# Decode kernel, attention plus MLP on one core: w1 becomes the first load and the hidden vector h is computed ahead of q

## The chip, the core and the metric

The kernel runs on one core of a Trainium2 chip. A core has five engines that run side by side, each with its own instruction queue: PE (matrix products into PSUM; "PEld" is its weight load), DVE (vector work), ACT (activations), POOL (here only constants), and SP, which here only issues transfers. Engines wait for each other by semaphores. Sixteen DMA engines move data between the chip's main memory and the on-chip memory SBUF. The metric is the time of one execution in microseconds (us), lower is better; the figure for a kernel is the median of several executions.

## What is computed

One token (x, 1024 values) goes through a layer norm, and the result xn feeds two branches whose sums are added to x:

```python
def _A_ref(x, k_cache, v_cache, wq, wo):      # 32 query heads, 4 kv heads, head size 128
    W = min(4096, max(256, Sk // 4))          # 4096: the last 4096 cached positions
    q = (x @ wq) ...                          # wq 1024 x 4096
    scores = einsum("bhqd,bhkd->bhqk", q, k) * (Dh ** -0.5)
    p = softmax(scores)
    o = einsum("bhqk,bhkd->bhqd", p, v)
    return o.reshape(B, Sq, Hq * Dh) @ wo     # wo 4096 x 1024
def _B_ref(x, w1, b1, w2, b2):
    h = gelu(layernorm(x) @ w1 + b1)          # w1 1024 x 3584
    return h @ w2 + b2                        # w2 3584 x 1024
xn = layernorm(x)
return x + _A_ref(xn, ...) + _B_ref(xn, ...)
```

All inputs are bfloat16. The six big ones take 38 MiB: wq 8, K 4, V 4, w1 7, w2 7, wo 8. Each is read once, and there is one token, so there is little arithmetic for each byte.

## The kernel before

**Where the data lies.** SBUF has four large tiles, which are used more than once. WA holds wq, and later w2; the end of WA, past w2, also holds the softmax numerators Pb and their transpose PT. W1 holds w1, and later rows 0 to 27 of wo (each "row" c is one slice of 128 x 1024). KT holds K, and later the last four rows of wo; V holds V. A small scratch tile of the gelu, HT32, lies in the last part of KT in the kernel before.

**Loads.** All large loads are issued by SP, one after the other (`load_rows`, L148-154, is one transfer per chunk): wq first (L156); then SP waits for a POOL constant (L187) and issues K in two halves (L188-192), w1 (L193), V in two halves (L194-198). Then it waits until PE has finished the product that gives q (L298) and issues w2 over wq (L299); then it waits until PE has finished h (L385) and issues wo in six chunks of 16, 8, 4, 2, 1 and 1 rows (L386-387). ACT issues x and b1 early (L169-170) and b2 (L245).

**Order of the work, in the order of each engine's queue.**

1. Layer norms (L240-278): xn goes to XNTb, the second norm to YTb.
2. `wide_product` (L281-294): 64 matmuls; each group of four runs side by side on four column strips of PE. With wq it gives q (L296).
3. q is copied, transposed and spread to QB (L301-324).
4. DVE transposes K in place, four pieces (L326-331); PE multiplies each piece by QB as it comes (scores, L339-348).
5. Softmax: maximum over PSUM (L352), a few tiny steps, exp on ACT (L367), the transpose PT on DVE (L370), sums and reciprocals (L373-381).
6. `wide_product` with w1 gives h (L384); DVE and ACT add b1, transpose, and apply gelu to GT (L389-413).
7. p times V (32 matmuls, L425-429), normalise (L432-440), spread to OT (L443-448); x and b2 are added by four matmuls (L453-455).
8. `bulk` (L457-461) multiplies one row of weights as two matmuls that run side by side. All 28 rows of w2 come first (L463-469), then rows 0 to 27 of wo (L476), then the last four rows in smaller pieces (L480-484).
9. DVE copies the sums (L488-492), adds (L495), and SP stores the result (L497).

PE takes its instructions in this order, whatever data is there.

## Time and profile before

| | |
|---|---|
| median of 3 executions | 101.97 us (101.0 to 102.63) |
| profiled execution, its own time | 100.91 us |
| its span, first to last instruction | 99.6 us |
| moved by DMA | 39.89 MB, mean 400 GB/s over the span |
| PE busy | 48.4 us (49%) |
| DVE busy | 38.8 us (39%) |
| ACT, POOL busy | 6.6 us, 9.6 us |

The profile comes from one execution. It has a page (busy shares, the span in 40 slices, DMA queues, the chain of work that ended last, the costliest groups of instructions, DMA issues) and a trace that can be asked for a timeline, for the waits of each engine, or for stretches of time ("windows"). L289 is line 289 of the kernel; "WA<-in_A_wq_dram" means that WA is written from that input. In the trace, the tile W1 is called W, and w1 and w2 both come as "in_B_w_dram". "PEclk" is the granted clock of PE, 1 being full speed.

### The profile page before, as it was taken

What the parts mean: (1) busy time and instruction counts of PE and PEld (TensorE: products, weight loads), DVE (VectorE), ACT (ScalarE), POOL (GpSimd) and SP (SyncE); (2) the same over time, 40 slices, a digit from 0 to 9 for tenths busy, and PEclk for the clock granted to TensorE, in tenths of its full rate; (3) what the DMA queues carried; (4) which work ended last, traced back from release to release, by engine and by line L of the source; (5) the groups of instructions that cost most, each with busy time, mean ns of one, the idle gap of its engine ahead of it and who ended that gap; (6) DMA issues with size and microseconds to landing.
All of it is one profiled execution on the core that took longest, in us unless ns stands there. A gap on an engine that the chain in (4) does not pass through costs nothing.

```text
span 99.6 us, 859 instructions
## 1 busy us (share of the span) xinstructions
PE 48.4 (49%) x350; PEld 19.3 (19%) x350; DVE 38.8 (39%) x50; ACT 6.6 (7%) x11; POOL 9.6 (10%) x40
## 2 busy tenths in 40 slices
PE   0000220008973419756071179990800899795760
PEld 0000220003321003112020133540700223241210
DVE  4000443000027999999918175498100000000052
ACT  0000236000022000000000620000000000000000
POOL 5777720000000000000000000000000000000000
PEclk9999999999999555599999755999555558999999
DMA  9199999939999889998699999999889999999920
GB/s 421 79 474 553 423 474 474 447 132 428 428 441 651 368 368 391 529 529 375 253 428 428 434 510 414 483 553 391 368 368 431 421 414 421 414 424 390 382 100 1
DMA packets 1906, 39.89 MB, mean 400 GB/s; under 512 B 224, under 2 KB 240, under 8 KB 624
## 3 DMA queue, kind: packets, MB, share of 16 engines
q1 hardware_dynamic: 1880, 39.85, 93.9%
q8 instruction: 2, 0.03, 0.1%
q10 hardware_dynamic: 24, 0.01, 0.0%
HBM read 39.86 MB, written 0.00 MB: 400 GB/s over the span
## 4 chain that ended last, share of the span: by engine, by line
DMA 52%; DVE 25%; PE 17%; ACT 2%; issue 1%; SPq 0%; DVEq 0%
DMA W<-in_A_wo_dram 30%; DMA WA<-in_A_wq_dram 22%; DVE KT L331 17%; PE PS L289 12%; DVE MX L352 2%; ACT WA L367 2%; PE PS L345 2%; DVE BULK L492 2%; DVE TQ L307 1%; PE PS L459 1%; DVE Q L302 1%; DVE QB L322 1%; SPq L150 0%; DVE ORow L495 0%; PE PS L311 0%
## 5 line engine op out<-in xcount | busy, mean ns | idle before, releaser
L331 DVE STREAM_TRANSPOSE KT<-KT 128x4096 bf16<-128x4096 bf16 x4 | 17.4, 4412 | 0.0
L345 PE MATMUL PS<-KT,QB 128*128 128x512 bf16 x32 | 9.7, 459 | 8.7 <-DVE KT L331 8.7
L459 PE MATMUL PS<-WA,GT 128*1 128x512 bf16 x56 | 9.0, 498 | 5.1 <-DMA WA<-in_B_w_dram 5.1
L492 DVE COPY BULK<-PS 1x256 f32<-1x256 f32 x4 | 1.7, 417 | 23.4 <-PE PS L459 23.3
L289 PE MATMUL PS<-WA,XNTb 128*32 128x512 bf16 x64 | 6.5, 592 | 7.9 <-DMA WA<-in_A_wq_dram 7.9
L459 PE MATMUL PS<-W,OT 128*1 128x512 bf16 x56 | 6.5, 378 | 2.5 <-DMA W<-in_A_wo_dram 2.5
L252 PE MATMUL PS<-XT,onesf 128*128 128x16 f32 x2 | 0.6, 386 | 11.7 <-DVE XT L249 11.7
L345 PEld LDWEIGHTS PS<-KT,QB 128*128 128x128 bf16 x32 | 3.3, 112 | 15.6 <-DVE KT L331 11.5
L302 DVE CAST Q<-PS 128x512 bf16<-128x512 f32 x1 | 0.7, 692 | 13.1 <-PE PS L289 13.1
L289 PE MATMUL PS<-W,YTb 128*32 128x448 bf16 x64 | 5.4, 525 | 0.0
L459 PEld LDWEIGHTS PS<-WA,GT 128*1 128x1 bf16 x56 | 2.9, 104 | 10.9 <-issue 9.3
L289 PEld LDWEIGHTS PS<-WA,XNTb 128*32 128x32 bf16 x64 | 2.4, 142 | 11.6 <-DMA WA<-in_A_wq_dram 8.0
L241 DVE STREAM_TRANSPOSE XT<-XB 128x256 bf16<-128x256 bf16 x1 | 0.6, 625 | 8.5 <-DMA XB<-in_A_x_dram 8.5
L427 PE MATMUL PS<-V,WA 128*64 128x512 bf16 x32 | 3.6, 380 | 0.0
L459 PEld LDWEIGHTS PS<-W,OT 128*1 128x1 bf16 x56 | 2.2, 83 | 6.9 <-DMA W<-in_A_wo_dram 2.8
L367 ACT ACTIVATE WA<-PS,NMB 128x2048 bf16<-128x2048 f32 x1 | 2.0, 1967 | 23.3 <-DVE NMB L365 23.3
L444 PE MATMUL PS<-ON,E 128*128 128x32 f32 x8 | 1.9, 404 | 2.8 <-DVE ON L439 2.8
L370 DVE STREAM_TRANSPOSE WA<-WA 128x2048 bf16<-128x2048 bf16 x1 | 2.3, 2312 | 2.1 <-ACT WA L367 2.1
L352 DVE TENSOR_REDUCE MX<-PS 128x1 f32<-128x2048 f32 x1 | 2.3, 2291 | 2.0 <-PE PS L345 2.0
L289 PEld LDWEIGHTS PS<-W,YTb 128*32 128x32 bf16 x64 | 2.2, 138 | 3.0 <-issue 2.8
L252 PEld LDWEIGHTS PS<-XT,onesf 128*128 128x128 f32 x2 | 0.5, 312 | 11.7 <-DVE XT L249 11.7
L215 POOL TENSOR_SCALAR_AFFINE_SELECT E<-E 32x512 f32<-32x512 f32 x4 | 2.5, 629 | 0.6
(87 smaller groups left out, 37.3 us busy)
## 6 DMA issues: line engine op xcount, KB each, us to landing
W<-in_B_w_dram SPq DMA_DIRECT2D x1, 7168.0 KB, 45.2
WA<-in_B_w_dram SPq DMA_DIRECT2D x1, 7168.0 KB, 48.1
KT<-in_A_k_cache_dram SPq DMA_DIRECT2D x2, 2048.0 KB, 25.6
V<-in_A_v_cache_dram SPq DMA_DIRECT2D x2, 2048.0 KB, 51.6
W<-in_A_wo_dram SPq DMA_DIRECT2D x1, 4096.0 KB, 23.5
W<-in_A_wo_dram SPq DMA_DIRECT2D x1, 2048.0 KB, 28.0
W<-in_A_wo_dram SPq DMA_DIRECT2D x1, 1024.0 KB, 30.0
KT<-in_A_wo_dram SPq DMA_DIRECT2D x1, 512.0 KB, 30.8
```

What stands on the lines that cost most here:

```text
L215: p(pool.affine_select(out=ap, in_=ap, pattern=[[1, 4], [-1, 128]], compare_op=ALU.not_equal, fill=1.0, base=0, channel_multiplier=4))
L289: last = pe.matmul(PS[32 * a:32 * a + 32, banks[b] * 512: banks[b] * 512 + n], lhsT=vec[:, k:k + 1].to_broadcast([128, 32]), rhs=weights[: ...
L302: d(dve.tensor_copy(Q4[:, 0:512], bank(4)))
L331: C["kt"].append(d(dve.transpose(KT[:, lo:lo + W], KT[:, lo:lo + W])))
L345: last = pe.matmul(bank(nb), lhsT=QB[:, G * 512 + c * 128:G * 512 + (c + 1) * 128], rhs=kg[:, c, 16 * nb:16 * nb + 16, :], start=False, st ...
L352: C["mx"] = d(dve.tensor_reduce(out=MX[:, :], in_=PS[:, 0:2048], axis=AX.X, op=ALU.max))
L367: C["exp"] = ACT.mark(act.activation(out=Pb, in_=PS[:, 0:2048], func=ACTF.Exp, bias=NMB[:, 0:1], scale=SCALE, accum_out=RS[:, 0:1]))
L370: C["PT"] = d(dve.transpose(PT, Pb))
L427: last = pe.matmul(PS[64 * q:64 * q + 64, 3 * 512:4 * 512], lhsT=PT[:, t * 64:(t + 1) * 64], rhs=vb[:, t], start=(t < 2), stop=(t >= 30))
L444: last = pe.matmul(bank(2, 352, 32), lhsT=E4[:, dq * 128:(dq + 1) * 128], rhs=ON[:, dq * 32:(dq + 1) * 32], start=(dq == 0), stop=(dq == 3))
L459: ins = pe.matmul(PS[32 * q:32 * q + 1, 6 * 512:7 * 512], lhsT=vec[:, c:c + 1], rhs=weights[:, lo + q * 512: lo + (q + 1) * 512], start=fi ...
L492: d(dve.tensor_copy(BULK[32 * a:32 * a + 1, :], PS[32 * q:32 * q + 1, lo:lo + 256]))
```

## The change

The order of the loads becomes w1, wq, K, V, w2, wo, and h with its gelu is computed before q. w1 takes the first place in SP's queue; wq is issued after the wait for the POOL constant, then K. The product h and the whole chain to GT move ahead of the product q, on PSUM banks 0 and 1 instead of 4 and 5. HT32 moves from KT to the same place in V, so SP waits for DVE's copy out of HT32 (C["ht"]) before it issues V. Then SP waits for q and issues w2, and behind it (h is long done) wo rows 0 to 27; it then waits for the scores (C["sc"]) and issues the last four rows of wo into KT. Everything from p times V on keeps its place and order.

```diff
-    HT32 = KT[:, 3 * W:3 * W + 2 * QW].bitcast(f32)
+    HT32 = V[:, 3 * W:3 * W + 2 * QW].bitcast(f32)
...
-    load_rows(WA, wq_p, WQ_CHUNKS, NQ, s_wq)
+    load_rows(W1, w1_p, W1_CHUNKS, F, s_w1)
...
     sp.wait_ge(POOL.sem, C["selq"])
+    load_rows(WA, wq_p, WQ_CHUNKS, NQ, s_wq)
     for G in range(NP):
         sp.dma_start(
             KT[:, G * PW:(G + 1) * PW],
...
-    load_rows(W1, w1_p, W1_CHUNKS, F, s_w1)
-    for G in range(NP):
-        sp.dma_start(
-            V[:, G * PW:(G + 1) * PW],
...
+    pe.wait_ge(DVE.sem, C["y"])
+    wide_product(W1, W1_CHUNKS, F, s_w1, YTb, QW // 2, [0, 1], "h")
+    dve.wait_ge(PE.sem, C["h"])
+    dve.wait_ge(s_b1, 16)
+    d(dve.tensor_tensor(
+        out=HW32[:, :].rearrange("p (b n) -> p b n", b=2),
+        in0=PS[:, 0:2 * 512].rearrange("p (b n) -> p b n", b=2)[:, :, 0:QW // 2],
+        in1=B1R[:, :].rearrange("p (b n) -> p b n", b=2), op=ALU.add))
+    dw()
+    d(dve.transpose(HT32[:, :].rearrange("p (c i) -> p c i", c=FC),
+                    HW32[:, :].rearrange("p (j c) -> p c j", c=FC)))
+    dw()
+    C["ht"] = d(dve.tensor_copy(HT[:, :], HT32[:, 0:QW:32]))
...
+    C["GT"] = d(dve.tensor_tensor(out=GT[:, :], in0=HT[:, :], in1=U2[:, :], op=ALU.mult))
+
+    sp.wait_ge(DVE.sem, C["ht"])
+    for G in range(NP):
+        sp.dma_start(
+            V[:, G * PW:(G + 1) * PW],
...
     wide_product(WA, WQ_CHUNKS, NQ, s_wq, XNTb, 512, [4, 5], "q")
 
     sp.wait_ge(PE.sem, C["q"])
     load_rows(WA, w2_p, W2_CHUNKS, D, s_w2)
+    sp.wait_ge(PE.sem, C["h"])
+    load_rows(W1, wo_p, WO_CHUNKS[:3], D, s_wo[:3])
...
     C["sc"] = PE.mark(last)
+    sp.wait_ge(PE.sem, C["sc"])
+    load_rows(KT, wo_p, WO_CHUNKS[3:], D, s_wo[3:], first=WO_BULK)
...
-    wide_product(W1, W1_CHUNKS, F, s_w1, YTb, QW // 2, [4, 5], "h")
-    sp.wait_ge(PE.sem, C["h"])
-    load_rows(W1, wo_p, WO_CHUNKS[:3], D, s_wo[:3])
-    load_rows(KT, wo_p, WO_CHUNKS[3:], D, s_wo[3:], first=WO_BULK)
...
```

The lines removed behind the last one shown are the same chain from L389 to L413 that is added further up.

More of the change, by code (lines that the diff above doesn't have):

```diff
@@ L192, in bass_parallel_sum__sliding_block_cached__mixer_channel_mlp__decode_kernel @@
         ).then_inc(s_k[G], 16)
-    load_rows(W1, w1_p, W1_CHUNKS, F, s_w1)
-    for G in range(NP):
-        sp.dma_start(
-            V[:, G * PW:(G + 1) * PW],
-            A_v_cache[0, 2 * G:2 * G + 2, SK - W:SK, :].rearrange("g (m b) d -> m g (b d)", m=64),
-        ).then_inc(s_v[G], 16)
     p(pool.memset(ML[:, :], NEG))
@@ L294, in wide_product @@
         C[name] = PE.mark(last)
+    pe.wait_ge(DVE.sem, C["y"])
[11 more added lines that the diff above has]
+    C["ht"] = d(dve.tensor_copy(HT[:, :], HT32[:, 0:QW:32]))
+    dw()
+    d(dve.tensor_tensor(out=U2[:, :], in0=HT[:, :], in1=HT[:, :], op=ALU.mult))
+    dw()
+    C["d_T"] = d(dve.scalar_tensor_tensor(out=U2[:, :], in0=U2[:, :], scalar=1.0 / 0.044715, in1=HT[:, :],
+                                          op0=ALU.add, op1=ALU.mult))
+    act.wait_ge(DVE.sem, C["d_T"])
+    C["a_sig"] = ACT.mark(act.activation(out=U2[:, :], in_=U2[:, :], func=ACTF.Exp,
+                                         scale=-GELU_C * 0.044715))
+    dve.wait_ge(ACT.sem, C["a_sig"])
+    d(dve.tensor_scalar(out=U2[:, :], in0=U2[:, :], scalar1=1.0, scalar2=None, op0=ALU.add))
+    dw()
+    d(dve.reciprocal(out=U2[:, :], in_=U2[:, :]))
+    dw()
+    C["GT"] = d(dve.tensor_tensor(out=GT[:, :], in0=HT[:, :], in1=U2[:, :], op=ALU.mult))
[3 more added lines that the diff above has]
+            V[:, G * PW:(G + 1) * PW],
+            A_v_cache[0, 2 * G:2 * G + 2, SK - W:SK, :].rearrange("g (m b) d -> m g (b d)", m=64),
+        ).then_inc(s_v[G], 16)
     wide_product(WA, WQ_CHUNKS, NQ, s_wq, XNTb, 512, [4, 5], "q")
@@ L381, in bass_parallel_sum__sliding_block_cached__mixer_channel_mlp__decode_kernel @@
         out=RR4[:, :].rearrange("o (q m) -> o q m", q=4), in_=LR[:, :].unsqueeze(1).to_broadcast([1, 4, 32])))
-    wide_product(W1, W1_CHUNKS, F, s_w1, YTb, QW // 2, [4, 5], "h")
-    sp.wait_ge(PE.sem, C["h"])
-    load_rows(W1, wo_p, WO_CHUNKS[:3], D, s_wo[:3])
-    load_rows(KT, wo_p, WO_CHUNKS[3:], D, s_wo[3:], first=WO_BULK)
-    dve.wait_ge(PE.sem, C["h"])
-    dve.wait_ge(s_b1, 16)
-    d(dve.tensor_tensor(
-        out=HW32[:, :].rearrange("p (b n) -> p b n", b=2),
-        in0=PS[:, 4 * 512:6 * 512].rearrange("p (b n) -> p b n", b=2)[:, :, 0:QW // 2],
-        in1=B1R[:, :].rearrange("p (b n) -> p b n", b=2), op=ALU.add))
-    dw()
-    d(dve.transpose(HT32[:, :].rearrange("p (c i) -> p c i", c=FC),
-                    HW32[:, :].rearrange("p (j c) -> p c j", c=FC)))
-    dw()
-    d(dve.tensor_copy(HT[:, :], HT32[:, 0:QW:32]))
-    dw()
-    d(dve.tensor_tensor(out=U2[:, :], in0=HT[:, :], in1=HT[:, :], op=ALU.mult))
-    dw()
-    C["d_T"] = d(dve.scalar_tensor_tensor(out=U2[:, :], in0=U2[:, :], scalar=1.0 / 0.044715, in1=HT[:, :],
-                                          op0=ALU.add, op1=ALU.mult))
-    act.wait_ge(DVE.sem, C["d_T"])
-    C["a_sig"] = ACT.mark(act.activation(out=U2[:, :], in_=U2[:, :], func=ACTF.Exp,
-                                         scale=-GELU_C * 0.044715))
-    dve.wait_ge(ACT.sem, C["a_sig"])
-    d(dve.tensor_scalar(out=U2[:, :], in0=U2[:, :], scalar1=1.0, scalar2=None, op0=ALU.add))
-    dw()
-    d(dve.reciprocal(out=U2[:, :], in_=U2[:, :]))
-    dw()
-    C["GT"] = d(dve.tensor_tensor(out=GT[:, :], in0=HT[:, :], in1=U2[:, :], op=ALU.mult))
     pe.wait_ge(DVE.sem, C["rr"])
```

## Prediction, made before the changed kernel ran

> **What bounds the kernel now.** I read the DMA row of the slices first, then the chain that ended last, the DMA issues, PE's timeline at the end, and last the granted clock in single microseconds. From the page, the queue that carries the big loads and the slices:

> ```profile
> DMA  9199999939999889998699999999889999999920
> ...
> q1 hardware_dynamic: 1880, 39.85, 93.9%
> ```

> The transfers are at work 93.9% of the span. (Slices 2 and 9 look empty because a large packet is booked at its start.) The chain in order of time says the same, and shows what lies between the loads:

> ```profile
> 0.81 21.95 DMA WA<-in_A_wq_dram
> ...
> 22.81 6.50 PE PS L289 x64
> ...
> 32.48 17.43 DVE KT L331 x4
> ...
> 64.50 30.04 DMA W<-in_A_wo_dram
> ...
> 94.58 1.05 PE PS L459 x8
> ```

> The end is set by wo's last big chunk; PE has some 1 us left when it lands. The chain's earlier part (wq, q, K's transposes, softmax) ends in plenty of time. The issues, with the time to landing:

> ```profile
> W<-in_B_w_dram SPq DMA_DIRECT2D x1, 7168.0 KB, 45.2
> WA<-in_B_w_dram SPq DMA_DIRECT2D x1, 7168.0 KB, 48.1
> ...
> V<-in_A_v_cache_dram SPq DMA_DIRECT2D x2, 2048.0 KB, 51.6
> W<-in_A_wo_dram SPq DMA_DIRECT2D x1, 4096.0 KB, 23.5
> ```

> With the issue times of the timeline (w1 5.51, w2 29.32, wo 63.64) the landings are: wq 22.8, w1 50.7, w2 77.4, first 16 rows of wo 87.2; V's slowest half, 53.7 us after 6.75, 60.5. They land in the order of issue: 8 MiB by 22.8, 19 by 50.7, 23 by 60.5, 30 by 77.4. The pace is 2.54 us per MiB from 22.8 to 50.7 (27.9 / 11) and 2.41 from 60.5 to 77.4 (16.9 / 7). So the queue never runs dry, and an order of loads alone changes only who waits. PE's timeline at the end shows how much slack the attention chain has:

> ```profile
> 63.83 3.64 PE L427 MATMUL PS<-V,WA 128*64 128x512 bf16 x32
> 70.23 1.92 PE L444 MATMUL PS<-ON,E 128*128 128x32 f32 x8 [2.76 <-DVE ON L439]
> 72.07 0.40 PE L454 MATMUL PS<-XB,SELX 128*32 128x256 bf16 x4
> 77.55 8.98 PE L459 MATMUL PS<-WA,GT 128*1 128x512 bf16 x56 [5.07 <-DMA WA<-in_B_w_dram]
> 87.25 3.62 PE L459 MATMUL PS<-W,OT 128*1 128x512 bf16 x32 [0.72 <-DMA W<-in_A_wo_dram]
> ```

> At 72.5 PE has all of attention behind it and waits 5.07 us for w2. That is the whole slack: attention may be some 5 us later before the end moves. Last, single microseconds in which the granted clock (third figure from the right) changes:

> ```profile
> 31.00:32.00 1.00, 0.56 (x6) 0.34 (x7) 0.52 (x2) 0.14 (x1) 0.00 (x0) 0.99 2.43 1049
> 42.00:43.00 1.00, 1.00 (x5) 0.44 (x4) 1.00 (x1) 0.00 (x0) 0.00 (x0) 0.89 1.98 860
> 55.00:56.00 1.00, 0.38 (x2) 0.29 (x2) 0.24 (x2) 0.26 (x1) 0.00 (x0) 0.94 0.96 410
> 62.00:63.00 1.00, 1.00 (x20) 0.44 (x16) 0.00 (x0) 0.00 (x0) 0.00 (x0) 0.64 1.99 860
> 69.00:70.00 1.00, 0.00 (x0) 0.00 (x0) 0.97 (x2) 0.00 (x0) 0.00 (x0) 0.77 1.19 516
> 83.00:84.00 1.00, 1.00 (x12) 0.40 (x10) 0.00 (x0) 0.00 (x0) 0.00 (x0) 0.91 0.68 295
> ```

> **The change, part by part.** I follow the queue of loads, then the chain behind wq; times are those of the profiled execution (span 99.6, own time 100.91, which is 1.31 more; the median 101.97 is 1.06 above that).

> *Loads.* w1 in wq's place has 1 MiB less: it lands at 22.8 - 2.4 = 20.4. wq, issued behind the wait for POOL (4.19, where K was issued), has w1 ahead of it until 20.4, so the wait costs nothing; without that cover it would cost 3.4 us. wq is then the 15th MiB: 20.4 + 8 x 2.41 to 2.54 = 39.7 to 40.7; between the 12th MiB (19 MiB at 50.7 less 7 at 2.54: 32.9) and the 19th I read 40.5, and take 40.4. K ends where w1 ended, 50.7. V now stands in SP's queue behind DVE's copy out of HT32. h: 64 matmuls of 448 columns took 5.43 with half of the clock for most of it; all at half clock, 16 groups of 0.37 are 6.0. So h ends by 26.4, and DVE's add, transpose and copy (1.09, 1.83, 0.19 and gaps, 3.2) let V go at 29.6, 21 us before K is through: free. w2 is queued behind V's wait and q's: issued at 47, before V is through at 60.5: free by 13 us. wo's 28 rows follow at once, 16 us earlier than before, but the queue takes them in turn; the last four rows wait for the scores (69.5, below) and are due after 94: free. The transfers end at 97 as before. b1's landing isn't in the trace; x took 8.5 us from its issue (2.14 to 10.6), b1 (issued 3.23) is wanted at 26, so I cost it nothing.

> *h and gelu.* They leave PE (5.43) and DVE (4.7, from 63.65 to 68.33) between the softmax and p times V, and lie now between 20.4 and 31, where both engines wait for wq. After them PE waits until 40.4, so q starts with the same slow matmuls as before.

> *The chain behind wq.* wq lands 40.4 - 22.8 = 17.6 later. Of the 17.6, the slack of 5.1 and the time that h took on PE's path are to be had; the rest is not hidden. From before, wq's landing to the end of the scores: 22.77 to 51.88, 29.1 (q 6.50, copies and transposes 3.2, K's transposes 17.43, last score group 1.9). K is there (50.7) when its second half is wanted (58.9). So scores end at 69.5. Softmax to the reciprocals ended at 61.28, 9.4 after the scores, and p times V can start 0.35 later (L417 to L427 took 0.31): 79.25. In the trace before it started at 63.83 because h was ahead of it, and h had brought the clock up. Now PE has nearly nothing to do for 9 us, so it starts at half clock: 16 pairs at 0.2275 (3.64 / 16) would be 3.64, at the slow pace of 0.427 (64 matmuls of L289 in groups of four, 6.46 / 16, with the last ones faster) 6.9; the clock came up 4.5 to 5.9 us after steady work began (58.2 to 62.7; 77.55 to 83.2; 37.05 to 42.2), which gives 5.8 to 6.4. I take 6.1: 85.35. Normalising 0.69 + 1.02 with gaps 1.8: 87.15. Spreading to OT (L444): 1.92 at a granted clock of 0.5, half of that is the lower bound; I take 1.4, between them, since the clock is in doubt: 88.55; the four matmuls of x and b2 add 0.15: 88.7. w2 landed at 77.4, so there is no wait left: 28 pairs at 0.213 (L459 with wo: 32 matmuls in 3.62, 16 x 0.213 + 0.2) are 6.0; with the clock down it is 8.98, the row before. I take 6.0, because PE has worked since 79: 94.7. wo's 28 rows, all landed by 94.6, are another 28 pairs, 6.0, and 0.2 to the last one's end: 100.9. Before, most of those 12 us lay beside wo's transfer; now nothing covers them. The last four rows (0.4 to 0.6) lie beside DVE's copies. Copies, add and store as before (95.65 to the span's end 99.6 is 4.0): 104.9. With 1.31: **106.2** against 100.91 of the same execution; loads set the first 40 of its 105 us, so of the 1.06 by which the median is above the profiled time I add 0.4: **106.6**.

> *The clock, weighed.* The rows place the changes at 31.98, 42.22, 55.88, 62.72, 69.54 and 83.18 (from the mean of 1 and 0.5 in each microsecond): all are multiples of 3.41 us apart. The stretch that ended at 69.54 had PE idle for its last 2.07 us only, and the clock went down; the one that ended at 45.64, idle for its last 2.0, kept it. Behind p times V there will be an idle of 1.8, then the small matmuls of L444. So the clock may go down there, and that depends on where the 3.41 us stretches fall. [...]

> **The rivals.** (1) *The loads stay the bound.* If attention were done in time, the end would be wo's landing as now: 102.0. For it: the load queue is unchanged in bytes, and h is gone from PE's path. The point from which it decides: PE has to start w2 12.2 before 95.6, at 83.4, so wq would have to land 5.3 sooner, at 35.1. That needs 15 MiB in 34.3 us, 2.29 each with no start-up, where the best stretch is 2.41 and the first 8 MiB took 2.74 each. Against.

> (2) *The clock goes down in the gap behind p times V.* L444 takes 1.92 (+0.5) and w2's loop starts at half speed: from +1.7 (one stretch of 3.41 at half speed) to +3.0 (8.98). With 2.3 of that, +2.8: 109.4. For it: the shut at 69.54; against: the stretch that ended at 45.64, and that 1.8 is the shortest gap of these.

> (3) *The loads share the engines* instead of going in turn, so that wq lands with K, at 50.7: +10.3, 116.9. Issued about 1 us apart they could; but K's half, w1 and V landed one behind the other before.

> **How the numbers follow.** Forecast 0.60, rival 1 0.06, rival 2 0.30, rival 3 0.04. The predicted time is the forecast's, 106.6. Low end: both loops begin with a stretch of 3.41 us, so that the clock is up after 3.41: q's product 5.1 for 6.46 (-1.4), p times V 5.2 for 6.1 (-0.9), and 0.5 for the scatter of the median: 103.8. High end: rival 2 at +3.5 (3.0 for w2's loop and 0.5), and the same 0.5: 110.6. Left out are rival 1, rival 3 and about 0.08 of the others, together 0.18. A measurement of this kernel can tell about 2%: below 99.9 is faster, above 104.0 slower. Of the forecast's 0.60 I give 0.04 to 103.8 to 104.0 and thereabouts: slower 0.56 + 0.30 + 0.04 = 0.90; same 0.04 + 0.05 = 0.09; faster 0.01, from rival 1 with a quick run of loads.

> **What would show it.** w1 landing near 20.4 and wq near 40.4; K's first transpose at 50.1; scores done at 69.5; p times V from 79.3 for about 6 us; w2's loop starting near 88.7 without a wait for a transfer; wo's loop without a wait either, and the chain that ended last through DVE's K transposes and PE L459, with no wo transfer in it. wo landed at 97 as before. The forecast is wrong if w2's loop starts before 84, if wq lands after 43, or if the wo loop still waits for its chunks.

## The result, and the profile after

The changed kernel takes 104.53 us (median of six executions, 103.96 to 108.53) against 101.48 (median of six, 100.83 to 102.63) for the kernel before: a ratio of 1.031, 95% interval 1.027 to 1.035. The ratio leaves out two executions of the changed kernel (107.18 and 108.53 us, at a mean granted clock of 0.80 and 0.79, where the others have 0.82 to 0.85), of which there is no trace. It is slower, by some 3.1 us. The profiled execution of the changed kernel took 104.27, with a span of 103.0; that of the kernel before 100.91 and 99.6. In the listings after the change, lines are numbered anew: K's transposes are L362, p times V is L428, the spread to OT L445, the `bulk` loops L460.

The page of the changed kernel, DMA row of the slices and load queue:

```profile
DMA  9888899999999999999999988998899999999000
...
q1 hardware_dynamic: 1880, 39.85, 90.8%
```

The bytes are the same, and the row now ends in three empty slices where it had one: the transfers are through and the kernel goes on without them. The chain that ended last, in order of time (start, us, what):

```profile
4.19 35.77 DMA WA<-in_A_wq_dram
...
40.01 5.73 PE PS L284 x60
...
48.91 17.44 DVE KT L362 x4
...
78.55 5.20 PE PS L428 x32
...
86.94 11.56 PE PS L460 x107
...
99.06 0.41 DVE BULK L493
```

Before, the largest link was wo's transfer (30.04 us) with 1.05 us of PE behind it. Now wo isn't in the chain; wq's landing, attention and then PE's two loops are. The DMA issues (size, us to landing):

```profile
W<-in_B_w_dram SPq DMA_DIRECT2D x1, 7168.0 KB, 19.8
WA<-in_B_w_dram SPq DMA_DIRECT2D x1, 7168.0 KB, 31.5
...
W<-in_A_wo_dram SPq DMA_DIRECT2D x1, 4096.0 KB, 40.8
```

With the issue times 0.81, 45.76 and 46.14 the landings are 20.6 for w1, 77.3 for w2 (before 77.4) and 86.9 for wo's first 16 rows (before 87.2). The loads as a whole are as quick as before. PE's timeline of the end:

```profile
78.48 5.25 PE L428 MATMUL PS<-V,WA 128*64 128x512 bf16 x32
85.64 1.08 PE L445 MATMUL PS<-ON,E 128*128 128x32 f32 x8 [1.91 <-DVE ON L440]
86.65 0.29 PE L455 MATMUL PS<-XB,SELX 128*32 128x256 bf16 x4
86.77 6.21 PE L460 MATMUL PS<-WA,GT 128*1 128x512 bf16 x56
92.81 5.78 PE L460 MATMUL PS<-W,OT 128*1 128x512 bf16 x52
```

w2's loop starts 9.2 us later than before, with no wait in brackets, and wo's loop follows without one. The waits of 5.07 and 0.72 for transfers that stood there before are gone: PE is late, not the data.

### The profile page after: what moved, and what is told of

The parts are those of the page before. It is cut to its first block, busy times and chain, and to the rows that moved or that the text cites. A ratio compares the mean times of both kernels' runs of the same rounds, so it can differ in the third digit from the quotient of the medians.

```text
span 103.0 us, 860 instructions
## 1 busy us (share of the span) xinstructions
PE 43.1 (42%) x350; PEld 18.7 (18%) x350; DVE 38.9 (38%) x50; ACT 6.6 (6%) x11; POOL 9.6 (9%) x40
## 3 DMA queue, kind: packets, MB, share of 16 engines
q1 hardware_dynamic: 1880, 39.85, 90.8%
## 4 chain that ended last, share of the span: by engine, by line
DMA 35%; DVE 29%; PE 27%; POOL 2%; issue 2%; ACT 2%; POOLq 0%; DVEq 0%
DMA WA<-in_A_wq_dram 35%; DVE KT L362 17%; PE PS L460 12%; PE PS L284 6%; PE PS L428 5%; DVE WA L403 2%; DVE MX L385 2%; ACT WA L400 2%; PE PS L376 2%; DVE BULK L493 1%; DVE TQ L338 1%; POOL SELQ L184 1%; PE PS L445 1%; DVE ON L440 1%; DVE RR L413 1%
## 5 line engine op out<-in xcount | busy, mean ns | idle before, releaser
L362 DVE STREAM_TRANSPOSE KT<-KT 128x4096 bf16<-128x4096 bf16 x4 | 17.4, 4413 | 0.0
L284 PE MATMUL PS<-WA,XNTb 128*32 128x512 bf16 x64 | 5.7, 533 | 14.6 <-DMA WA<-in_A_wq_dram 14.6
L284 PE MATMUL PS<-W,YTb 128*32 128x448 bf16 x64 | 4.7, 465 | 6.6 <-DMA W<-in_B_w_dram 6.6
L493 DVE COPY BULK<-PS 1x256 f32<-1x256 f32 x4 | 1.7, 417 | 12.2 <-PE PS L460 12.1
L460 PE MATMUL PS<-WA,GT 128*1 128x512 bf16 x56 | 6.2, 379 | 0.0
L460 PE MATMUL PS<-W,OT 128*1 128x512 bf16 x56 | 6.2, 379 | 0.0
L428 PE MATMUL PS<-V,WA 128*64 128x512 bf16 x32 | 5.3, 500 | 0.0
L295 DVE TENSOR_TENSOR HW<-PS,B1R 128x896 f32<-128x896 f32 x1 | 1.1, 1091 | 9.9 <-PE PS L284 9.9
L400 ACT ACTIVATE WA<-PS,NMB 128x2048 bf16<-128x2048 f32 x1 | 2.0, 1967 | 23.5 <-DVE NMB L398 23.5
L460 PEld LDWEIGHTS PS<-W,OT 128*1 128x1 bf16 x56 | 2.4, 84 | 3.6
L460 PEld LDWEIGHTS PS<-WA,GT 128*1 128x1 bf16 x56 | 2.4, 84 | 3.4
L428 PEld LDWEIGHTS PS<-V,WA 128*64 128x64 bf16 x32 | 2.2, 143 | 2.6 <-issue 1.9
L436 DVE TENSOR_TENSOR HW<-PS,MG 128x512 f32<-128x512 f32 x1 | 0.7, 692 | 5.1 <-PE PS L428 5.1
## 6 DMA issues: line engine op xcount, KB each, us to landing
W<-in_B_w_dram SPq DMA_DIRECT2D x1, 7168.0 KB, 19.8
WA<-in_B_w_dram SPq DMA_DIRECT2D x1, 7168.0 KB, 31.5
KT<-in_A_k_cache_dram SPq DMA_DIRECT2D x2, 2048.0 KB, 43.2
V<-in_A_v_cache_dram SPq DMA_DIRECT2D x2, 2048.0 KB, 28.9
W<-in_A_wo_dram SPq DMA_DIRECT2D x1, 4096.0 KB, 40.8
W<-in_A_wo_dram SPq DMA_DIRECT2D x1, 2048.0 KB, 45.7
```

Of the source, the lines that this page charges most:

```text
L284: last = pe.matmul(PS[32 * a:32 * a + 32, banks[b] * 512: banks[b] * 512 + n], lhsT=vec[:, k:k + 1].to_broadcast([128, 32]), rhs=weights[: ...
L295: d(dve.tensor_tensor(out=HW32[:, :].rearrange("p (b n) -> p b n", b=2), in0=PS[:, 0:2 * 512].rearrange("p (b n) -> p b n", b=2)[:, :, 0:Q ...
L362: C["kt"].append(d(dve.transpose(KT[:, lo:lo + W], KT[:, lo:lo + W])))
L400: C["exp"] = ACT.mark(act.activation(out=Pb, in_=PS[:, 0:2048], func=ACTF.Exp, bias=NMB[:, 0:1], scale=SCALE, accum_out=RS[:, 0:1]))
L428: last = pe.matmul(PS[64 * q:64 * q + 64, 3 * 512:4 * 512], lhsT=PT[:, t * 64:(t + 1) * 64], rhs=vb[:, t], start=(t < 2), stop=(t >= 30))
L460: ins = pe.matmul(PS[32 * q:32 * q + 1, 6 * 512:7 * 512], lhsT=vec[:, c:c + 1], rhs=weights[:, lo + q * 512: lo + (q + 1) * 512], start=fi ...
```

## The experiments

Theory A is that of the prediction: wq's late landing pushes attention behind the loads, and PE's two loops, some 12 us that used to lie beside wo's transfer, then set the end. Theory B: the loads themselves got slower. Theory C: h's early place in PE's order does it, not the loads. Theory D, added later: only wq's place counts. "Span" is that of the profiled execution, "ratio" is to the kernel before, and the load bound is the span at which the landing of wo sets the end, 99.6 us in the kernel before.

### Shorter loops: half of w2, and one row of w2

```diff
-        for _ in range(n):
+        for _ in range(n // 2):        # first kernel; range(1) in the second
             bulk(WA, GT, c, c * D, c == 0, False)
```

> The changed kernel, but PE multiplies only the first 14 of w2's 28 rows (the output lacks the rest; every load stays). Theory A (PE's two loops behind attention, 6.0 us each, are uncovered and set the end): 14 pairs of 0.216 us less on the path, span 103.0 - 3.0 = 100.0; PE's wait for wo's chunks is still none or a few tenths. Theory B (the loads got slower, 387 GB/s on average for 400, and set the end): span 103.0, unchanged, with PE waiting for wo.

Measured: span 100.6, ratio 1.004 (1.000 to 1.008). The 3.1 us are nearly all back; PE's only wait behind them is 0.22 for the last row. In this execution q's product took 6.37 and p times V 5.69 (5.70 and 5.25 in the changed kernel's). Of these 1.1 us, 0.3 is made up by wq, which landed sooner, and 0.2 by a shorter softmax step; the rest is the 0.6 above the expected 100.0.

> The changed kernel, but PE multiplies only one of w2's 28 rows (the output lacks the rest; every load stays). Theory A: the wo loop starts 27 pairs earlier (5.8 us), but now it must wait for wo's 28th row, which lands near 94.8; the end goes back to the load bound of the kernel before, span 99.6 to 99.8 (3.3 less, not 5.8). Theory B: span 103.0. If wo lands later than before, the floor found here is above 99.8.

Measured: span 99.5, ratio 1.000 (0.999 to 1.001). PE's timeline of this kernel:

```profile
86.52 0.38 PE L460 MATMUL PS<-WA,GT 128*1 128x512 bf16 x2
87.07 3.62 PE L460 MATMUL PS<-W,OT 128*1 128x512 bf16 x32 [0.17 <-DMA W<-in_A_wo_dram]
91.87 1.89 PE L460 MATMUL PS<-W,OT 128*1 128x512 bf16 x16 [1.18 <-DMA W<-in_A_wo_dram]
94.38 1.03 PE L460 MATMUL PS<-W,OT 128*1 128x512 bf16 x8 [0.62 <-DMA W<-in_A_wo_dram]
```

The brackets are back: wo's chunks are waited for again, 0.2 us ahead of the times of the kernel before (87.25, 92.05, 94.58). So taking 5.8 us off PE gains 3.5 of span, down to the load bound and no further. Theory B falls: with every load in place and the new order, the load bound is where it was.

### The same work without the gap

w2's loop moves ahead of the spread to OT:

```diff
+    pe.wait_ge(DVE.sem, C["GT"])
+    for j, n in enumerate(W2_CHUNKS):
...
     pe.wait_ge(DVE.sem, C["on"])
     for dq in range(4):
...
-    pe.wait_ge(DVE.sem, C["GT"])
-    for j, n in enumerate(W2_CHUNKS):
...
```

> The changed kernel with w2's loop moved ahead of the spread to OT, so that it fills the 1.9 us in which PE waits for DVE's normalising. Nothing is left out. Theory A: that wait is on the path that sets the end, so the span falls by 1.9 less the wait for OT's copy (0.3): 101.4. Theory B: 103.0.

Measured: span 102.2, ratio 1.020 (1.016 to 1.025), 1.0% under the changed kernel's. The wait of 1.91 has gone and 0.35 for OT's copy has come, as expected, but p times V took 6.47 in the profiled execution (5.25 in the changed kernel's), so its span shows only half of the gain. The direction is A's; the size is uncertain, as the two profiled executions had mean granted clocks of 0.81 and 0.847.

### wq in chunks

```diff
-WQ_CHUNKS = [8]
+WQ_CHUNKS = [4, 2, 1, 1]
```

> The changed kernel with wq's load cut into chunks of 4, 2, 1 and 1 rows, so that most of q's product is done before the last of wq lands. Theory A: the product ends about 1.0 after wq's landing instead of 5.8, everything behind it moves up by up to 4.8 and the load bound takes over: span 99.6 to 99.9. Theory B: 103.0, unchanged, as no byte is moved earlier. K's first half (landed near 45.5) would hold K's transposes back at the earliest from 45.5, which is later than the 44.1 that this asks for: then 99.7 to 100.0.

Measured: span 100.0, ratio 1.006 (1.003 to 1.009). PE's timeline (q's product in four parts, and the loops):

```profile
30.00 3.60 PE L284 MATMUL PS<-WA,XNTb 128*32 128x512 bf16 x32 [4.42 <-DMA WA<-in_A_wq_dram]
...
40.98 1.04 PE L284 MATMUL PS<-WA,XNTb 128*32 128x512 bf16 x8 [1.45 <-DMA WA<-in_A_wq_dram]
...
83.77 6.21 PE L460 MATMUL PS<-WA,GT 128*1 128x512 bf16 x56
89.81 6.21 PE L460 MATMUL PS<-W,OT 128*1 128x512 bf16 x56
95.90 0.40 PE L483 MATMUL PS<-KT,OT 128*32 128x256 bf16 x8
96.54 0.29 PE L483 MATMUL PS<-KT,OT 128*32 128x256 bf16 x4 [0.24 <-DMA KT<-in_A_wo_dram]
```

w2's loop starts 3.0 us sooner than in the changed kernel, at 83.77, and the last rows of wo wait for their transfer: the crossing point is here, as the prediction's first rival placed it (83.4). DVE waited 0.7 us for K's first half, so K holds attention as soon as wq no longer does.

### Only the order of the loads

The kernel before with the new order of loads, h at its old place:

```diff
-    load_rows(WA, wq_p, WQ_CHUNKS, NQ, s_wq)
+    load_rows(W1, w1_p, W1_CHUNKS, F, s_w1)
...
     sp.wait_ge(POOL.sem, C["selq"])
+    load_rows(WA, wq_p, WQ_CHUNKS, NQ, s_wq)
     for G in range(NP):
...
-    load_rows(W1, w1_p, W1_CHUNKS, F, s_w1)
```

> The kernel before with only the order of the loads changed (w1, wq, K, V, w2, wo); h stays where it was, between the softmax and p times V, and wo still waits for h. Theory A: wq's late landing moves the chain by 17.2; h's product and gelu are on it again, h ends near 80.3, w2's loop starts near 86.5 and wo is issued only at 80.3, when the queue has run dry at 77.4, so wo ends near 102 and the span is near 106. Theory C (the early h in PE's order does the harm, not the loads): span at or below 99.6.

Measured: span 105.5, ratio 1.056 (1.046 to 1.067). The order alone does more harm than the whole change; the early h takes some of it back. Theory C falls. PE's timeline, and SP's:

```profile
74.50 4.88 PE L289 MATMUL PS<-W,YTb 128*32 128x448 bf16 x64
...
79.62 3.64 PE L427 MATMUL PS<-V,WA 128*64 128x512 bf16 x32
86.04 1.08 PE L444 MATMUL PS<-ON,E 128*128 128x32 f32 x8 [2.78 <-DVE ON L439]
...
87.17 7.89 PE L459 MATMUL PS<-WA,GT 128*1 128x512 bf16 x56
94.90 6.49 PE L459 MATMUL PS<-W,OT 128*1 128x512 bf16 x56
```

```profile
45.46 0.34 SPq L150 DMA_DIRECT2D WA<-in_B_w_dram  x1
79.43 1.28 SPq L150 DMA_DIRECT2D W<-in_A_wo_dram  x3
```

w2's loop starts at 87.17, 0.4 later than in the changed kernel, and runs 1.7 longer. And wo is issued only at 79.43, when h is done, 2.3 after w2's landing at 77.2: the queue of loads runs dry. The chain that ended last takes this second way, but DVE's copies of the sums behind PE's loops end at the same time:

```profile
81.81 21.03 DMA KT<-in_A_wo_dram
...
103.30 0.42 DVE ORow L495
```

```profile
101.43 1.76 DVE L492 COPY BULK<-PS 1x256 f32<-1x256 f32 x4 [14.08 <-PE PS L459]
```

wo's last landing at 102.84 leads to PE's last row at 103.21; the copies end at 103.19. So the late issue of wo cost at most the 0.3 by which the wo loop is longer (6.49 for 6.21). The rest of what the early h buys is PE's: 0.4 of start and 1.7 in w2's loop. With h late, DVE has its gelu still to finish behind p times V and begins to normalise 1.0 after its end (84.24 for 83.26; 0.1 in the changed kernel), so PE's wait is 2.78 for 1.91, and the granted clock goes down at 88.16.

### How late attention may be: part of w1 ahead of wq

The kernel before, w1 in two chunks, the first ahead of wq, the second where w1 was:

```diff
-W1_CHUNKS = [8]
+W1_CHUNKS = [4, 4]        # [6, 2] in the second kernel
...
+    load_rows(W1, w1_p, W1_CHUNKS[:1], F, s_w1[:1])
     load_rows(WA, wq_p, WQ_CHUNKS, NQ, s_wq)
...
-    load_rows(W1, w1_p, W1_CHUNKS, F, s_w1)
+    load_rows(W1, w1_p, W1_CHUNKS[1:], F, s_w1[1:], c0=4)        # c0=6
```

> The kernel before, with the first 4 of w1's 8 rows (3.5 MiB) loaded ahead of wq and nothing else moved: attention comes about 8.5 us later, w2's loop would start near 81. If the slack is the 5.1 us for which PE waits for w2: +3.4, span 103.0. If it reaches to the start of w2's loop at 83.4, as the loops can catch up with wo: span 99.6, unchanged. Theory C expects no change either.

Measured: span 99.7, ratio 0.999 (0.996 to 1.003). wq landed 8.5 us later (31.29 for 22.81), the spread to OT began 7.1 later (77.36 for 70.23), w2's loop began 0.9 later (78.49 for 77.55), and the end didn't move. A slack of 5.1 would have cost 0.9 or more, outside the interval.

> The kernel before, with the first 6 of w1's 8 rows (5.25 MiB) loaded ahead of wq: attention comes about 12.7 us later, w2's loop would start near 85.2. Slack up to 83.4: span 99.6 + 1.8 = 101.4. Slack of 5.1: +7.6, 107.2. Theory C (the place of h, not the loads): 99.6.

Measured: span 101.7, ratio 1.014 (1.007 to 1.021). The number is that of a slack up to 83.4, and the cause isn't. PE's timeline:

```profile
83.41 6.21 PE L460 MATMUL PS<-WA,GT 128*1 128x512 bf16 x56
89.45 3.62 PE L460 MATMUL PS<-W,OT 128*1 128x512 bf16 x32
94.11 1.89 PE L460 MATMUL PS<-W,OT 128*1 128x512 bf16 x16 [1.04 <-DMA W<-in_A_wo_dram]
96.62 1.03 PE L460 MATMUL PS<-W,OT 128*1 128x512 bf16 x8 [0.61 <-DMA W<-in_A_wo_dram]
```

w2's loop began at 83.41, in time, and PE waits for wo. Its chunks are 2 us late because h, which lies behind the softmax here, let wo be issued only at 75.67. Windows of 1 us of this kernel (last two columns: DMA share and GB/s):

```profile
75.00:76.00 1.00, 1.00 (x20) 0.54 (x10) 0.32 (x1) 0.00 (x0) 0.00 (x0) 1.00 0.01 0
76.00:77.00 1.00, 1.00 (x12) 0.49 (x10) 0.97 (x2) 0.00 (x0) 0.00 (x0) 1.00 1.18 328
```

In the first of them hardly a packet begins. In the kernel with 4 rows, where wo was issued at 70.76, the same window has a share of 1.15 and 492 GB/s. w2 landed at 77.6, 1.9 us after wo's issue, yet wo's first chunk landed 11.6 after w2 (89.2), where the kernel before has 9.8. So this run tells nothing of PE's slack beyond 83.4, but shows a second price of lateness.

### PE kept busy during the softmax

```diff
+    for _ in range(10):        # then 8 and 12, ahead of the two later waits
+        pe.matmul(bank(4), lhsT=SELQ[:, 0:128], rhs=TQ[:, 0:512], start=True, stop=True)
     pe.wait_ge(DVE.sem, C["mx"])
```

> The changed kernel with 30 idle matmuls (10 + 8 + 12, into an unused bank, nothing reads them) in PE's waits during the softmax, so that the clock should still be up when p times V starts. If the granted clock is what made p times V 5.2 us instead of 3.6: it takes 3.6 and the step before it 0.4 for 0.6, span 103.0 - 1.8 = 101.2. If not (say, V's reads or the loads slow it): 103.0 or more, since the idle matmuls may hold the small steps up by some tenths.

Measured: span 101.6, ratio 1.018 (1.011 to 1.026). PE's timeline:

```profile
78.39 0.38 PE L424 MATMUL PS<-identf,RR 1*128 1x1 f32 x2 [0.62 <-DVE RR L417]
78.70 3.64 PE L434 MATMUL PS<-V,WA 128*64 128x512 bf16 x32
```

p times V takes 3.64 and the step before it 0.38, as in the kernel before, where the granted clock reads 1.00 from 63 to 68 us. In the changed kernel it is 0.50 from 71.54 to 81.78, and the two take 5.25 and 0.58: what differs is PE's clock, not V or the loads. (q's product took 6.56 here, 0.9 more than in the changed kernel's execution, so the span shows less than the full gain.)

### Both mends together

wq in chunks, and w2's loop in the gap: the diffs of the third and the fourth kernel.

> The changed kernel with both mends: wq's load in chunks of 4, 2, 1 and 1 rows, and w2's loop moved into PE's wait behind p times V. Theory A: the loops have caught up with the loads; w2's loop starts near 80.9 and the wo loop waits for wo's chunks again, so the end is the load bound, span 99.6, a ratio of 1.00 to the kernel before, and no less, since no byte is saved. If the new order of loads costs something of its own, it is left over here, above 99.6.

Measured: span 100.0, ratio 1.0035 (1.0005 to 1.0065). w2's loop starts at 80.74, and the wo loop waits for its chunks again (0.51, 0.60). The loss is gone but for 0.3 us, and nothing is won. The kernel with one row of w2 has the new order too and stands at 1.000, so the 0.3 isn't shown to be the order's. The chunks of wq and the full loop of w2 are what differs between the two, and no run tells them apart.

### w1 ahead of K, with wq first

```diff
     load_rows(WA, wq_p, WQ_CHUNKS, NQ, s_wq)
+    load_rows(W1, w1_p, W1_CHUNKS, F, s_w1)
...
-    load_rows(W1, w1_p, W1_CHUNKS, F, s_w1)
```

> The kernel before with wq still first, but w1 ahead of K (wq, w1, K, V, w2, wo), and h at its old place. Tells whether it is wq's landing alone that counts. Theory A (whatever attention needs last): q is ready at 32.5 as before, but K's first half lands only near 45.5, so K's transposes run from 45.5 for 32.5 and end near 63; scores 64.9, h near 76, w2's loop from about 84, span 100.0 to 101.7. Theory D (only wq's place counts, since K is wanted after it): 99.6.

Measured: span 103.0, ratio 1.025 (1.018 to 1.031). DVE's and PE's timelines:

```profile
44.67 17.42 DVE L331 STREAM_TRANSPOSE KT<-KT 128x4096 bf16<-128x4096 bf16 x4 [12.76 <-DMA KT<-in_A_k_cache_dram]
```

```profile
82.58 1.92 PE L444 MATMUL PS<-ON,E 128*128 128x32 f32 x8 [2.77 <-DVE ON L439]
84.43 0.40 PE L454 MATMUL PS<-XB,SELX 128*32 128x256 bf16 x4
84.62 8.31 PE L459 MATMUL PS<-WA,GT 128*1 128x512 bf16 x56
```

Theory D falls: with wq as early as before, attention now waits 12.76 us for K. The span is above the expected range by 1.3. w2's loop starts at 84.62, 0.6 later than said, and the clock went down in the wait of 2.77, so that the spread takes 1.92 for 1.08 and w2's loop 8.31 for 6.21: 2.9 us, the prediction's second rival seen at work.

## Why the prediction was right

The forecast was 106.6, in a range of 103.8 to 110.6; 104.53 was measured. The mechanism is the forecast's, and the runs bear it out: shortening the loops, starting them sooner, or bringing wq's product forward each gives time back, and none gets below the load bound, 99.5 to 100.0. The size was too large: a rise of 4.6 (106.6 for the 101.97 known then) was forecast, and 3.1 came. Step by step:

- **Loads.** w1 20.6 (said 20.4), wq 39.96 (40.4), V's issue 28.63 (29.6), w2 77.3 (77.4). The issues behind the new waits cost nothing, as said.
- **wq to the end of the scores.** 28.3 (said 29.1). q's product took 5.73 for the 6.50 copied from the profile before: the clock came up 4.2 us after its start (at 44.22), and before some 5.7 after it, an estimate from its weight loads, which come 0.43 apart until 28.33.
- **Scores to p times V.** 10.2 (said 9.75). The one step that was under-sized: the tiny matmuls of the softmax took 0.58 each at a granted clock of 0.50 (71.54 to 81.78) where the rows before had 0.38 (L396 and L418).
- **p times V.** 5.2 (said 6.1, bounds 3.64 and 6.9). That PE would start it slow, with no h just ahead of it, was right: the clock reads 0.50 until 81.78, 3.3 after its start, and with PE kept busy ahead of it, it took 3.64.
- **Spread to OT.** 1.08 (said 1.4): the clock stayed up (1.00 from 82 to 102).
- **The loops.** 12.3 from w2's start to the last one's end (said 12.2), with no wait.
- **Sum.** Span 103.0 (said 104.9). The 1.9 are 0.4 of wq's landing, 0.8 in q, 0.9 in p times V and 0.3 in the steps behind it, less 0.5 in the softmax. Three of these are one thing: where in PE's work the clock changes. The phase of the profile before was copied as if it were a cost. The measured p times V is that of the low end of the range (5.2), which lets the clock come up after 3.41; it came up after 3.3. The runs' profiles differ in this (q's product took 5.30 to 6.56 with wq in one piece), so how near the forecast came is in part luck.

Three of its readings were off, though none of them moves the sum. That "the clock came up 4.5 to 5.9 us after steady work began" isn't what its three pairs of times give: they are 4.5, 5.6 and 5.2, so that p times V would be 5.8 to 6.3, and the 6.1 stays between. That "an order of loads alone changes only who waits" leaves out issues that wait for a product: with the new order alone, wo was issued 2.3 after the queue was empty. "That is the whole slack" put it at the 5.07 us of waiting for w2; the kernel with 4 rows of w1 ahead shows that attention may end later than that, as PE's loops catch up with wo, and the fourth kernel has the crossing near 83.8 for the 83.4 of the first rival. **Rival 1** (the loads stay the bound) failed where it was said to: w2's loop would have had to start by 83.4 and started at 86.8. **Rival 2** (the clock goes down behind p times V) didn't come in the profiled execution of the changed kernel, nor in the four other profiles with a wait of 1.91 there (the spread took 1.08 in each); whether it comes in some of its executions that weren't profiled stays open. With a wait of 2.77 it came in three of four (w2's loop 7.89, 7.90, 8.31, and 6.21). **Rival 3** (loads sharing the engines) is out: wq landed at 39.96, K's halves near 45.8 and 50.4.

## What to carry to other kernels

When the loads are the bound, their order saves no byte; it only decides which computation has its data first. Put first what the longest dependent chain needs (here wq and K, with 47 us from wq's landing to OT), and last what needs the least work after landing (here wo, with some 1 us of PE behind its last big chunk); an idle engine that is filled early (with h) pays only as far as something waits for that work or for the buffer that it frees. A wait for data is not the whole slack: work it out from the end backwards, as the point at which the remaining compute no longer fits beside the remaining transfers.

## What the runs showed of the chip

```profile
30.00:31.00 1.00, 0.00 (x0) 0.00 (x0) 0.10 (x1) 0.00 (x0) 0.00 (x0) 0.79 0.00 0
44.00:45.00 1.00, 1.00 (x24) 0.41 (x16) 0.00 (x0) 0.00 (x0) 0.00 (x0) 0.89 0.95 393
51.00:52.00 1.00, 0.00 (x0) 0.00 (x0) 1.00 (x1) 0.00 (x0) 0.00 (x0) 0.53 1.19 508
57.00:58.00 1.00, 0.34 (x2) 0.13 (x2) 1.00 (x2) 0.00 (x0) 0.00 (x0) 0.56 1.11 475
71.00:72.00 1.00, 0.44 (x2) 0.44 (x2) 0.47 (x2) 0.00 (x0) 0.00 (x0) 0.77 1.72 745
81.00:82.00 1.00, 1.00 (x8) 0.47 (x6) 0.00 (x0) 0.00 (x0) 0.00 (x0) 0.61 1.14 492
```

Between the changes the windows read 0.50 or 1.00. A mean of 0.89 is 0.22 us at 0.50, so the change is at 44.22; likewise 30.58, 51.06, 57.88, 71.54 and 81.78. From one to the next it is 13.64, 6.84, 6.82, 13.66 and 10.24 us, or 4, 2, 2, 4 and 3 times 3.41; in the trace before, from 31.98 on, it is 3, 4, 2, 2 and 4 times. The same 64 matmuls of q's product took from 5.30 to 6.56 us in the kernels that load wq in one piece. In the changed kernel they took 5.70, and the clock came up 4.2 us after their start; groups of four came 0.43 apart before that and 0.21 after it. From these paces alone it would have come up 3.4 after their start for the 5.30 (w2's loop in the gap) and 5.9 for the 6.56 (PE kept busy): an estimate. One profile's number for this burst of matmuls after an idle stretch is thus good to about 1 us, by the 1.3 between the two.

A wait of 2.77 ahead of the spread was followed by the clock's going down in three of four profiles, as in the kernel before at 69.54. In only one of the three (w1 ahead of K, at 82.02) did it go down in the wait itself; in the other two it went down at 79.08 (4 rows) and 88.16 (order alone), when PE had been at work again for 1.7 and 2.1 us.

The windows' clock reads 1.00 up to 30 us in both kernels, though h's product at 20.74 took 4.67, where its 16 groups would take some 3.0 at full speed, an estimate from the 0.213 us of a pair of 512 columns in wo's loop (448 of 512 columns): until the first change that column doesn't tell the pace.

And in these runs the load queue had to be fed some time ahead: wo, issued 1.9 us before w2's landing, landed 1.8 us late (the kernel with 6 rows of w1 ahead); issued 6.6 before, it lost nothing (4 rows). Where the queue was empty or nearly so at its issue, wo's first chunk took 13.3 to 13.5 us to land (w1 ahead of K, 6 rows, order alone), against the 9.8 that it needs behind w2 in a full queue. The difference, some 3.6 us, is an estimate of the lead that such a load needs here.
